# Weight sign and softmax-sum steps moved between engines, and the value product of a group issued in one piece

## The chip, the cores and the metric

The kernel runs on one core of one Trainium2 chip. Five engines matter. TensorE (PE in the profile, with its weight loads as PEld) multiplies matrices out of SBUF into PSUM. VectorE (DVE) and ScalarE (ACT) work elementwise on SBUF and PSUM. GpSimd (POOL) works elementwise on SBUF only. SyncE (SP) issues most of the DMAs. The metric is the device time of one execution in microseconds; lower is better.

## The reference

Three stages follow one another. In the kernel's sizes: 4 batches, 8 heads, sequence 576, head dimension 64; then 2304 tokens of width 512.

```python
scores = scale * np.matmul(q, k.transpose(0, 1, 3, 2)) + bias   # bias: a small MLP of log distances
attn = np.exp(scores - np.max(scores, axis=-1, keepdims=True))
attn = attn / (np.sum(attn, axis=-1, keepdims=True) + 1e-09)
x = np.matmul(attn, v)                       # heads side by side: (2304, 512)
h = x @ w_in                                 # d_ff 2048
g = (a0 + a1*h + a2*h*h + a3*h*h*h) / (1 + |b0|*|h| + |b1|*h*h + 1e-6)
x = g @ w_out
h = np.maximum(np.maximum(x @ w1, x @ w2), x @ w3)   # d_ff 768
out = h @ w_out2
```

The six weight matrices of the last two stages arrive as 64-bit floats; everything else is 32-bit.

## The kernel before

**Attention.** A pair of heads `p` (four of them) of batch `b` is cut into five row blocks `t` of 128 rows (the last has 64 rows of each head, so one block serves both heads). One `(b, t, p)` is a unit; there are 80. `attn_tick(n)` (L719) issues, in the order of the list `A2`, one step each for several units at once: `scores` of unit n (L223, PE, into two PSUM buffers called `wide`, one for each head), `reduce_min` of unit n (L258, DVE: adds the bias, scales, finds the row minimum; it frees the `wide` buffer), `expo` of unit n (L264, ACT, with the row sum), `normalise` of unit n-1 (L266), `transposes` of unit n-2 (L287, PE, into `bank` buffers, of which there are four) and their copies to SBUF on ACT and DVE. For 14 of the 16 pairs `(b, p)` the units run t = 0 to 4 in two groups, [0, 1] and [2, 3, 4]. I call these five ticks a cycle.

**Softmax sum.** `normalise` adds 1e-9 to the two sums `st` (128x2), takes the reciprocal in place and spreads it to a 128x128 tile `rb`, which PE transposes into `tt` (L303) as the last matmul of the unit's transposes. All three steps are on DVE (`NE` is 'd').

**Value product.** When the last block of a group has been transposed, `attn_v` (L323) is queued for the next ticks: ten matmuls (`av`) whose moving operand is the whole group, 256 or 320 columns. They are cut into pieces of one tick each by `cuts` (L765): for a group of two blocks j = 0..2 and then 3..4, for a group of three j = 0..1, 2..3 and 4. `attn_store` (L340) then scales the result out of its bank on DVE.

**Weights.** A weight of 64-bit floats is loaded as pairs of 32-bit words, `low` and `high` (L371). `rebias` (L379) multiplies the high word, read as a 32-bit float, by 2^-112 on ACT and shifts the low word right by 29 on DVE; `join` (L385) makes `(high << 3) | low` on DVE; `sign` (L390) takes the sign bit of the high word and ors it in, on DVE. `parts` (L402) then splits the result into a rounded and a remaining part, on ACT and on POOL or DVE. Sixteen weights `wi` are narrowed during attention and written back to DRAM (`wnwin`), sixteen `wo` are prepared around the start of the first feed-forward block, and 24 of the last stage (`m0`, `m1`, `m2`, `mo`) from the last feed-forward block on, one for each step. That makes 56 such weights in all.

**Feed-forward.** `ffn_tick` (L669) runs 16 steps for each of five token blocks. A step has 12 matmuls `ph`, 12 matmuls `y` of the step two before, the rational function on ACT and DVE (`rat_poly`, `rat_inv`, `rat_newton`) and its split `gs` (ACT, then POOL, L507), followed by one step of the weight pipeline. `moe_tick` (L813) runs the last stage.

**What sets the order.** In attention from tick 8 on, PE and SP run in the order of the program, while the order of DVE, ACT and POOL is chosen by a scheduler at build time. In the feed-forward stage DVE, too, runs in the order of the program. Each engine executes its own queue strictly in that order.

Of the kernel before, what the change touches and what calls it, by code (L numbers as in the profile page):

```python
# [13 lines left out]
ALU = mybir.AluOpType  # L14
# [23 lines left out]
def tile_attention_moe(  # L38
# [328 lines left out]
    def weight_stages(src, name, n, packed=False, lo_eng=pool, narrow=None):  # L367
# [11 lines left out]
        def rebias():  # L379
            if wide_:  # L380
                low, high = box["r"][:, :, 0], box["r"][:, :, 1]
                act.activation(f32(high), f32(high), AF.Copy, scale=REBIAS)
                dve.tensor_scalar(low, low, 29, None, ALU.logical_shift_right)  # L383

        def join():  # L385
            if wide_:
                low, high = box["r"][:, :, 0], box["r"][:, :, 1]
                dve.scalar_tensor_tensor(low, high, 3, low, ALU.logical_shift_left, ALU.bitwise_or)  # L388

        def sign():  # L390
            if wide_:
                low, high = box["r"][:, :, 0], box["r"][:, :, 1]
# [3 lines left out]
                dve.scalar_tensor_tensor(res, high, SIGN, low, ALU.bitwise_and, ALU.bitwise_or)  # L396
# [498 lines left out]
```

## Time and profile before

| | |
|---|---|
| median of three runs | 1100.29 us (1100.19 to 1100.94) |
| profiled execution, its own time | 1100.39 us |
| its span, first to last instruction | 1098.6 us |
| around the span | 1.8 us |
| PE busy | 1040.5 us (95%) |
| DVE busy | 750.8 us (68%) |
| ACT busy | 620.7 us (57%) |
| POOL busy | 418.9 us (38%) |

The shares are means over stages with different limits. Attention fills about 45 to 360 us of the span (after a first part that builds the bias), the feed-forward blocks 360 to 800, and the last stage 800 to the end. A busy PE in this profile is not PE at its full rate, since a matmul that waits in the middle counts as busy, so starts of groups on the timeline say more than the busy share.

### The profile page before, as it was taken

To read this page: it belongs to the slowest core of one execution; us is meant where nothing else is said; L and a number is where in the kernel's file an instruction comes from. 1 tells how busy PE (TensorE), PEld (TensorE's weight loads), DVE (VectorE), ACT (ScalarE), POOL (GpSimd) and SP (SyncE) were. 2 spreads that over 40 slices of the span, in tenths; PEclk is the share of its full clock that TensorE was granted. 3 is DMA by queue.
4 is the path that set the end of the run, shared out by engine and by line. 5 is a ranking of instruction groups with operands and counts; after the bars stand their busy time and mean duration, and the time that the engine had idled before them with its cause. 6 is when DMAs were issued, how large, how long until landed. Compare 5 with 4: busy or idle time off the path is not lost. (4 is left out here: it accounts for less than half of the span.)

```text
span 1098.6 us, 16477 instructions
## 1 busy us (share of the span) xinstructions
PE 1040.5 (95%) x5996; PEld 811.5 (74%) x5996; DVE 750.8 (68%) x1512; ACT 620.7 (57%) x1226; POOL 418.9 (38%) x409
## 2 busy tenths in 40 slices
PE   5699999999999879999999999999999999999998
PEld 2247677677776557878889788777688788888887
DVE  8496899899998899877789777799984211111111
ACT  5686667676778667766678766777632211211111
POOL 7614555455486534322233323243442330211111
PEclk9799999999999889999999999999999999999999
DMA  7486845255455422010020200223233200201010
GB/s 261 158 314 217 291 153 168 99 204 173 155 160 174 136 103 77 1 58 1 1 77 1 78 1 1 78 77 115 77 118 131 77 1 1 77 1 58 1 39 20
DMA packets 43393, 107.94 MB, mean 98 GB/s; under 512 B 4784, under 2 KB 11184, under 8 KB 43312
## 3 DMA queue, kind: packets, MB, share of 16 engines
q1 hardware_dynamic: 38128, 96.27, 26.1%
q10 hardware_dynamic: 5184, 10.62, 2.5%
q8 instruction: 47, 0.77, 0.3%
q14 instruction: 34, 0.28, 0.1%
HBM read 77.90 MB, written 28.97 MB: 97 GB/s over the span
## 5 line engine op out<-in xcount | busy, mean ns | idle before, releaser
L459 PE MATMUL p<-ys,wm 128*128 128x512 f32 (+1 forms) x1080 | 228.8, 369 | 2.8 <-POOL wm L413 1.8
L459 PE MATMUL ph<-xs,wwi 128*128 128x512 f32 (+1 forms) x960 | 217.8, 375 | 5.7 <-ACT at L748 3.5
L459 PEld LDWEIGHTS p<-ys,wm 128*128 128x128 f32 x1080 | 188.4, 188 | 39.4 <-POOL wm L413 2.2
L459 PE MATMUL y<-gs,wwo 128*128 128x512 f32 (+1 forms) x905 | 207.7, 374 | 7.9 <-POOL gs L507 7.2
L459 PEld LDWEIGHTS ph<-xs,wwi 128*128 128x128 f32 x960 | 170.4, 191 | 41.8 <-POOL xs L451 3.8
L507 POOL TENSOR_TENSOR gs<-g,gs 128x512 fp32r<-128x512 f32 (+1 forms) x80 | 102.2, 1277 | 234.6 <-ACT gs L506 160.2
L459 PEld LDWEIGHTS y<-gs,wwo 128*128 128x128 f32 x905 | 157.3, 188 | 46.4 <-POOL gs L507 13.7
L264 ACT ACTIVATE e<-e,st 128x576 f32<-128x576 f32 x144 | 111.5, 775 | 59.3 <-DVE st L258 53.4
L551 POOL TENSOR_TENSOR h2s<-mx,h2s 128x512 fp32r<-128x512 f32 (+1 forms) x30 | 35.9, 1197 | 226.9 <-ACT h2s L550 226.9
L258 DVE CUSTOM_DVE_ANT_0 e<-s,bias 128x576 f32<-128x576 f32 x144 | 104.0, 751 | 16.3 <-PE s L233 11.7
L547 DVE TENSOR_TENSOR mx<-p,mx 128x512 f32<-128x512 f32 (+1 forms) x30 | 19.1, 637 | 140.0 <-PE p L459 136.1
L480 ACT ACTIVATE s<-ph,keep 128x512 f32<-128x512 f32 (+1 forms) x80 | 49.3, 617 | 75.9 <-PE ph L459 74.1
L233 PE MATMUL s<-k,qs 128*128 128x288 f32 x512 | 86.3, 308 | 4.6 <-DVE st L258 2.8
L550 ACT CAST h2s<-mx 128x512 fp32r<-128x512 f32 (+1 forms) x30 | 17.3, 578 | 128.9 <-DVE mx L548 128.9
L296 PEld LDWEIGHTS tp<-ident,e 128*128 128x128 f32 x576 | 62.5, 142 | 35.6 <-issue 17.1
L296 PE MATMUL tp<-ident,e 128*128 128x128 f32 x576 | 82.0, 282 | 1.0 <-DVE at L317 0.8
L482 DVE SCALAR_TENSOR_TENSOR g<-g,keep,s 128x512 f32<-128x512 f32 (+1 forms) x80 | 55.2, 690 | 36.6 <-ACT g L481 36.0
L338 PE MATMUL av<-at,v 128*64 128x320 f32 (+3 forms) x576 | 77.7, 392 | 1.3 <-DVE st L269 0.7
L565 PE MATMUL o<-wmo,h2s 128*128 128x512 f32 x324 | 78.6, 390 | 0.0
L233 PEld LDWEIGHTS s<-k,qs 128*128 128x128 f32 x512 | 70.6, 189 | 9.0 <-DVE st L258 3.7
L185 PE MATMUL pb<-h,keep 128*32 128x288 f32 x576 | 48.7, 442 | 23.8 <-ACT h L173 22.6
L487 ACT ACTIVATE s<-g,keep 128x512 f32<-128x512 f32 (+1 forms) x80 | 52.7, 659 | 31.7 <-DVE g L482 31.6
(102 smaller groups left out, 1665.0 us busy)
## 6 DMA issues: line engine op xcount, KB each, us to landing
bias_d<-bo ACTq DMA_DIRECT2D x36, 288.0 KB, 2.9
kr<-in_k SPq DMA_DIRECT2D x16, 576.0 KB, 5.1
qr<-in_q SPq DMA_DIRECT2D x16, 576.0 KB, 5.6
bias<-bias_d SPq DMA_DIRECT2D x16, 576.0 KB, 5.3
wrm<-in_m SPq DMA_DIRECT2D x18, 512.0 KB, 3.6
wrwin<-in_wi SPq DMA_DIRECT2D x16, 512.0 KB, 4.4
wrwo<-in_wo SPq DMA_DIRECT2D x16, 512.0 KB, 3.7
v<-in_v SPq DMA_DIRECT2D x8, 576.0 KB, 4.5
```

Of the source, the lines that this page charges most:

```text
L185: pe.matmul(pb[32 * c:32 * c + 32, x, :HS], lhsT=hw_sb, rhs=hs[c][:, x * HS:(x + 1) * HS], start=True, stop=True,)
L233: pe.matmul(pt[:, x, :HS], lhsT=qs[:, u, t * P:(t + 1) * P], rhs=ks[u][:, w, x * HS:(x + 1) * HS], start=w == 0, stop=w == 1,)
L258: dve.tensor_tensor_reduce(out=dst, in0=src, in1=bs, op0=ALU.add, op1=ALU.min, scale=-0.125, scalar=3.0e38, accum_out=st[:, u:u + 1],)
L264: act.activation(et[:, u], et[:, u], AF.Exp, bias=st[:, u:u + 1], scale=-1.0, accum_out=st[:, 2 + u:3 + u])
L296: pe.transpose(tp[:, j * P:(j + 1) * P], flat[:, 640 * u + j * P:640 * u + (j + 1) * P], ident)
L338: pe.matmul(po[r, :n], lhsT=l, rhs=m, start=j == 0, stop=j == 4, skip_group_check=True)
L459: pe.matmul(po, lhsT=wpart(key, a, k), rhs=rhs, start=first and i == 0, stop=last and i == 2)
L480: act.activation(s, ph, AF.Abs, scale=B0)
L482: dve.scalar_tensor_tensor(q, q, B1, s, ALU.mult, ALU.add)
L487: act.activation(s, q, AF.Ln, bias=qcol)
L507: pool.tensor_tensor(t[1], u, f32(t[0]), ALU.subtract)
L565: pe.matmul(po, lhsT=h[:, a, tt * P:(tt + 1) * P], rhs=w[c], start=j == 0 and i == 0, stop=j == NF2 - 1 and i == 2,)
```

## The change

Three edits are made together. First, `rebias` uses the activation Prelu with slope -2^32 for negative values instead of Copy: a negative high word comes out positive and 2^32 times larger, which sets exactly the bit that the shift by three moves into the sign. `sign` falls away, and `join` writes the final result; for a narrowed weight the store follows `join` at once, so its list of stages is one shorter. Second, in `normalise` the addition of 1e-9 and the spreading to `rb` go to POOL; the reciprocal stays on DVE between them. Third, `CUT2` and `CUT3` become 1, so each group's ten `av` matmuls stand in one tick.

```diff
...
-'CUT2': 2, 'CUT3': 3,
+'CUT2': 1, 'CUT3': 1,
...
-SIGN = -(1 << 31)
+TOSIGN = -2.0 ** 32
...
-        dve.tensor_scalar(r, r, 1e-9, None, ALU.add)
+        pool.tensor_scalar(r, r, 1e-9, 0.0, ALU.add, ALU.add)
+        dve.reciprocal(r, r)
         rb = sb.tile([P, 2, 64], F32, tag="rb", name=f"rb{b}_{t}_{p}", bufs=4)
-        dve.reciprocal(r, r)
-        evac(KN["NE"], (rb, r.unsqueeze(2).to_broadcast([P, 2, 64])))
+        pool.tensor_copy(rb, r.unsqueeze(2).to_broadcast([P, 2, 64]))
...
-                act.activation(f32(high), f32(high), AF.Copy, scale=REBIAS)
+                act.activation(f32(high), f32(high), AF.Prelu, scale=REBIAS, alpha=TOSIGN)
                 dve.tensor_scalar(low, low, 29, None, ALU.logical_shift_right)
...
         def join():
-            if wide_:
-                low, high = box["r"][:, :, 0], box["r"][:, :, 1]
-                dve.scalar_tensor_tensor(low, high, 3, low, ALU.logical_shift_left, ALU.bitwise_or)
-
-        def sign():
             if wide_:
...
-                dve.scalar_tensor_tensor(res, high, SIGN, low, ALU.bitwise_and, ALU.bitwise_or)
+                dve.scalar_tensor_tensor(res, high, 3, low, ALU.logical_shift_left, ALU.bitwise_or)
                 box["r"] = f32(res)
...
-            return [load, rebias, join, lambda: (sign(), put())]
-        return [load, rebias, lambda: (join(), sign()), parts]
+            return [load, rebias, lambda: (join(), put())]
+        return [load, rebias, join, parts]
...
-        eq += st[1:3] + [st[0] for st in early[i + 2:i + 3]] + st[3:]
+        eq += st[1:2] + [st[0] for st in early[i + 2:i + 3]] + st[2:]
```

On PE, at the first two ticks of the pair b = 1, p = 3 (`s` are scores, `tp` and `tt` transposes; the numbers behind a name are t and p, and for `s` and `tp` the half), this stood in a row before:

```order
L233 MATMUL s_0_3_0_2457<-k_3_0_2207,qs_3_2206 128x288 x4
L233 MATMUL s_0_3_1_2462<-k_3_1_2208,qs_3_2206 128x288 x4
L338 MATMUL av_0_2_2467<-at_0_2_2221,v_2_1744 64x256 x6
L296 MATMUL tp_3_2_0_2474<-ident,e_3_2_2359 128x128 x4
L296 MATMUL tp_3_2_1_2479<-ident,e_3_2_2359 128x128 x4
L302 MATMUL tt_3_2_2484<-ident,e_3_2_2359 128x128
L303 MATMUL tt_3_2_2484<-ident,rb_3_2_2433 128x128
L233 MATMUL s_1_3_0_2504<-k_3_0_2207,qs_3_2206 128x288 x4
L233 MATMUL s_1_3_1_2509<-k_3_1_2208,qs_3_2206 128x288 x4
L338 MATMUL av_0_2_2467<-at_0_2_2221,v_2_1744 64x256 x2
L338 MATMUL av_0_2_2467<-att_0_2_2222,v_2_1744 64x256 x2
L296 MATMUL tp_4_2_0_2518<-ident,e_4_2_2405 128x128 x4
```

And this stands there now:

```order
L233 MATMUL s_0_3_0_2464<-k_3_0_2214,qs_3_2213 128x288 x4
L233 MATMUL s_0_3_1_2469<-k_3_1_2215,qs_3_2213 128x288 x4
L296 MATMUL tp_3_2_0_2474<-ident,e_3_2_2359 128x128 x4
L296 MATMUL tp_3_2_1_2479<-ident,e_3_2_2359 128x128 x4
L302 MATMUL tt_3_2_2484<-ident,e_3_2_2359 128x128
L303 MATMUL tt_3_2_2484<-ident,rb_3_2_2442 128x128
L233 MATMUL s_1_3_0_2504<-k_3_0_2214,qs_3_2213 128x288 x4
L233 MATMUL s_1_3_1_2509<-k_3_1_2215,qs_3_2213 128x288 x4
L296 MATMUL tp_4_2_0_2514<-ident,e_4_2_2402 128x128 x4
```

No `av` stands between scores and transposes in these two ticks any more; all ten matmuls of group [0, 1] now stand in the tick of t = 4 and all ten of [2, 3, 4] in the tick of t = 2 of the next pair, so that the ticks of t = 0, 1 and 3 have none.

On POOL, for the same place (`qs` and `k` are the split of the next pair's queries and keys, `e` the copy of the last block's tail), this stood in a row before:

```order
L138 TENSOR_SCALAR qs_0_2440<-qr_0_2219 128x1024
L144 TENSOR_SCALAR k_0_0_2441<-kr_0_2217 128x576
L141 TENSOR_TENSOR qs_0_2440<-qr_0_2219,qs_0_2440 64x512 x2
L275 COPY e_4_2_2405<-e_4_2_2405 128x64
L147 TENSOR_TENSOR k_0_0_2441<-kr_0_2217,k_0_0_2441 128x576
```

And this stands there now:

```order
L272 COPY rb_2_2_2391<-st_2_2_2309 128x128
L138 TENSOR_SCALAR qs_0_2447<-qr_0_2226 128x1024
L144 TENSOR_SCALAR k_0_0_2448<-kr_0_2224 128x576
L269 TENSOR_SCALAR st_3_2_2360<-st_3_2_2360 128x2
L141 TENSOR_TENSOR qs_0_2447<-qr_0_2226,qs_0_2447 64x512 x2
L269 TENSOR_SCALAR st_4_2_2403<-st_4_2_2403 128x1
L275 COPY e_4_2_2402<-e_4_2_2402 128x64
L147 TENSOR_TENSOR k_0_0_2448<-kr_0_2224,k_0_0_2448 128x576
L272 COPY rb_3_2_2442<-st_3_2_2360 128x128
L272 COPY rb_4_2_2491<-st_4_2_2403 128x128
```

The spread `rb` of unit t = 3, which PE needs in the first tick of the next pair, now stands behind three large splits that lie between it and its own addition.

On DVE, at the same ticks (`e`, `st` are the reductions of unit t, `xs` the store of a group), this stood in a row before:

```order
L258 ISA e_0_3_2455,st_0_3_2456<-s_0_3_0_2457,bias_3_1319 128x576
L258 ISA st_0_3_2456 128x1
L269 TENSOR_SCALAR st_4_2_2406<-st_4_2_2406 128x1
L271 RECIPROCAL st_4_2_2406<-st_4_2_2406 128x1
L317 COPY rb_4_2_2490<-st_4_2_2406 128x128
L258 ISA e_1_3_2502,st_1_3_2503<-s_1_3_1_2509,bias_3_1361 128x576
```

And this stands there now:

```order
L258 ISA e_0_3_2462,st_0_3_2463<-s_0_3_0_2464,bias_3_1317 128x576
L258 ISA st_0_3_2463 128x1
L270 RECIPROCAL st_4_2_2403<-st_4_2_2403 128x1
L258 ISA e_1_3_2502,st_1_3_2503<-s_1_3_1_2509,bias_3_1367 128x576
```

Of the three steps only the reciprocal is left on DVE, and it waits for POOL.

## Rows read from the trace of the kernel before

**Rows 1.** By stretch: length, busy (count) of PE, PEld, DVE, ACT, POOL; clock, DMA.

```profile
200.00:350.00 150.00, 149.03 (x1099) 109.85 (x1097) 135.11 (x383) 112.52 (x265) 90.72 (x108) 1.00 0.50 167
...
355.00:405.00 50.00, 39.73 (x169) 28.36 (x170) 44.36 (x71) 33.87 (x62) 22.82 (x17) 0.86 0.41 136
...
700.00:795.00 95.00, 90.09 (x375) 69.03 (x373) 89.81 (x134) 69.50 (x120) 36.79 (x25) 1.00 0.31 100
```

**Rows 2.** PE timeline of a steady attention cycle: start, duration, engine, line, group.

```profile
230.83 1.53 PE L243 MATMUL s<-k,qtail 128*128 128x512 f32 x8
...
235.28 1.52 PE L338 MATMUL av<-at,v 128*64 128x256 f32 x12
236.73 1.09 PE L296 MATMUL tp<-ident,e 128*128 128x128 f32 x8
...
237.79 1.30 PE L233 MATMUL s<-k,qs 128*128 128x288 f32 x8
239.03 0.65 PE L338 MATMUL av<-at,v 128*64 128x256 f32 x4
...
240.19 0.66 PE L296 MATMUL tp<-ident,e 128*128 128x128 f32 x4
...
240.82 1.29 PE L233 MATMUL s<-k,qs 128*128 128x288 f32 x8
...
247.87 1.53 PE L243 MATMUL s<-k,qtail 128*128 128x512 f32 x8
```

**Rows 3.** Groups by line and shape, 100 to 340 us: count, busy us, mean ns.

```profile
L264 ACT ACTIVATE e<-e,st 128x576 f32<-128x576 f32 x120 | 92.9, 775 | 54.8 <-DVE st L258 49.0 <-DVE st L269 4.3 <-ACT att L315 1.3
L258 DVE CUSTOM_DVE_ANT_0 e<-s,bias 128x576 f32<-128x576 f32 x121 | 87.0, 750 | 11.6 <-PE s L233 7.3 <-PE s L243 3.6 <-issue 0.4
...
L147 POOL TENSOR_TENSOR k<-kr,k 128x576 fp32r<-128x576 f32 x26 | 37.6, 1447 | 1.2
L141 POOL TENSOR_TENSOR qs<-qr,qs 64x512 fp32r<-64x512 f32 x26 | 35.3, 1376 | 1.1
...
L317 DVE COPY rb<-st 128x128 f32<-128x128 f32 x69 | 30.7, 444 | 2.3
...
L269 DVE TENSOR_SCALAR st<-st 128x2 f32<-128x2 f32 x53 | 19.6, 369 | 0.4 <-ACT e L264 0.4
```

**Rows 4.** Timelines of DVE and POOL at one normalisation.

```profile
243.73 1.05 DVE L269 TENSOR_SCALAR st<-st 128x2 f32<-128x2 f32 x1
...
243.71 1.04 POOL L138 TENSOR_SCALAR qs<-qr 128x1024 fp32r<-128x1024 f32 x1
```

**Rows 5.** PE timeline, the longest of eight waits between 100 and 200 us.

```profile
114.06 1.47 PE L233 MATMUL s<-k,qs 128*128 128x288 f32 x8 [1.74 <-DVE st L258]
```

**Rows 6.** Timelines of ACT and PE around the first feed-forward steps.

```profile
363.76 0.68 ACT L412 CAST wwo<-wrwo 128x512 fp32r<-128x512 f32 x1 [2.44 <-DVE wrwo L396]
...
389.30 1.22 PE L459 MATMUL y<-gs,wwi 128*128 128x512 f32 x2 [4.78 <-ACT gs L506]
```

**Rows 7.** PE and DVE timelines of the last feed-forward block.

```profile
700.31 2.96 PE L459 MATMUL y<-gs,wwo 128*128 128x512 f32 x12
...
705.84 2.95 PE L459 MATMUL y<-gs,wwo 128*128 128x512 f32 x12
...
784.64 3.31 PE L459 MATMUL y<-gs,wwo 128*128 128x512 f32 x12
...
722.13 0.75 DVE L494 SCALAR_TENSOR_TENSOR g<-g,keep,s 128x512 f32<-128x512 f32 x1
...
728.01 0.75 DVE L494 SCALAR_TENSOR_TENSOR g<-g,keep,s 128x512 f32<-128x512 f32 x1
...
735.60 0.75 DVE L494 SCALAR_TENSOR_TENSOR g<-g,keep,s 128x512 f32<-128x512 f32 x1
```

**Rows 8.** Two lines by themselves: count, then min/median/max ns.

```profile
L396 DVE SCALAR_TENSOR_TENSOR wrm<-wrm x18: 681/693/1669, 713.1 to 841.2; 128x512 int32<-128x512 int32 x18
...
L507 POOL TENSOR_TENSOR gs<-g,gs x15: 1290/1539/1818, 703.0 to 790.6; 128x512 fp32r<-128x512 f32 x15
```

More of the change, by code (lines that the diff above doesn't have):

```diff
@@ L29 @@
 TW = 1148
-KN = {'NSLOT': 35, 'NRAW': 3, 'NRAWX': 2, 'NATT': 4, 'HB': 0, 'NE': 'd', 'FP': 2, 'BL': 4, 'T4': 0, 'LSP': 1, 'KX': 4, 'HT': 'ss', 'EVP': 'da', 'TTP': 'dda', 'NXS': 4, 'EARLY': 0, 'NM0': 8, 'MAN': 2, 'MANF': 3, 'A1': ['b', 'T', 'sc', 'st', 'r0', 'av', 'b', 'b', 'b', 'sq', 'n', 'r1', 'p2', 'v0', 'v1', 'e0', 'e1'], 'A2': ['sc', 'av', 'p1', 'T', 'r1', 'r0', 'n', 'st', 'p2', 'sq', 'e0', 'e1', 'v0', 'v1'], 'LL': 10, 'SL': 4, 'LL0': 9, 'SL0': 4, 'SQ': [2, 1, 1], 'CUT2': 2, 'CUT3': 3, 'WS': 9, 'WE': 70, 'WT': 61, 'XT': 8, 'XA': 3, 'XB': 8, 'F': ['g2a', 'g2d', 'h', 'g1a', 'w', 'g2p', 'g1d', 'g1p', 'y', 'x', 'g3'], 'LOW': 4, 'LOM': 3, 'LOI': 0, 'GHI': 'dve', 'GLO': 'dve', 'BED': 8, 'BE0': 16, 'NU1': 'pool', 'XE': ['act', 'pool'], 'WR': 1, 'YSP': 'act', 'LAG': 2, 'EV1': 'dve', 'XSE': 'act', 'STQ': 'sp', 'PUQ': 'sp', 'NB0': 0, 'HP': 0, 'SB': 2, 'XLA': 3, 'XLB': 6, 'XSA': 11, 'YL': 10, 'YS': 14, 'WLOW': 1}
+KN = {'NSLOT': 35, 'NRAW': 3, 'NRAWX': 2, 'NATT': 4, 'HB': 0, 'NE': 'd', 'FP': 2, 'BL': 4, 'T4': 0, 'LSP': 1, 'KX': 4, 'HT': 'ss', 'EVP': 'da', 'TTP': 'dda', 'NXS': 4, 'EARLY': 0, 'NM0': 8, 'MAN': 2, 'MANF': 3, 'A1': ['b', 'T', 'sc', 'st', 'r0', 'av', 'b', 'b', 'b', 'sq', 'n', 'r1', 'p2', 'v0', 'v1', 'e0', 'e1'], 'A2': ['sc', 'av', 'p1', 'T', 'r1', 'r0', 'n', 'st', 'p2', 'sq', 'e0', 'e1', 'v0', 'v1'], 'LL': 10, 'SL': 4, 'LL0': 9, 'SL0': 4, 'SQ': [2, 1, 1], 'CUT2': 1, 'CUT3': 1, 'WS': 9, 'WE': 70, 'WT': 61, 'XT': 8, 'XA': 3, 'XB': 8, 'F': ['g2a', 'g2d', 'h', 'g1a', 'w', 'g2p', 'g1d', 'g1p', 'y', 'x', 'g3'], 'LOW': 4, 'LOM': 3, 'LOI': 0, 'GHI': 'dve', 'GLO': 'dve', 'BED': 8, 'BE0': 16, 'NU1': 'pool', 'XE': ['act', 'pool'], 'WR': 1, 'YSP': 'act', 'LAG': 2, 'EV1': 'dve', 'XSE': 'act', 'STQ': 'sp', 'PUQ': 'sp', 'NB0': 0, 'HP': 0, 'SB': 2, 'XLA': 3, 'XLB': 6, 'XSA': 11, 'YL': 10, 'YS': 14, 'WLOW': 1}
 REBIAS = 2.0 ** -112
-SIGN = -(1 << 31)
+TOSIGN = -2.0 ** 32
 QC = 1.0 + 1e-6
```

## The prediction

> **What bounds the kernel now.** I read the busy time by stretch first, then the PE timeline of the stretches where PE is full, then the engine that ends PE's waits where it is not.
>
> From 200 to 350 us PE is busy 149.03 of 150 us and DVE 135.11, while POOL has 90.72 [rows 1]. One attention cycle of five units takes 247.87 - 230.83 = 17.04 us [rows 2], and its groups follow one another without a gap. So in steady attention PE sets the time, and what DVE sheds there gains nothing by itself. DVE is close behind, though, and its small operations cost more than their size: the addition takes 369 ns and the spreading to `rb` 444 ns on average [rows 3].
>
> It is different in three places. Between 100 and 200 us PE waits eight times, 4.8 us in sum, mostly on DVE; the longest wait is 1.74 us for the reduction that frees a score buffer [rows 5]. From 355 to 405 us PE is busy for only 39.73 of 50 us and DVE for 44.36 [rows 1]; ACT waits 2.44 us for a `sign`, and PE 4.78 us for a chain that has come through DVE [rows 6]. In the last feed-forward block, 700 to 795 us, DVE has 89.81 of 95 us [rows 1]. A step at PE's pace is 705.84 - 700.31 = 5.53 us, and 14 steps would be 77.4; they take 784.64 - 700.31 = 84.33 [rows 7], so 6.9 us are lost. DVE's own steps there are 5.88 us, and every third is 735.60 - 728.01 = 7.59 [rows 7].
>
> **The change part by part.**
>
> *The sign in the last block.* One operation of 0.69 us (median) [rows 8] leaves DVE per step. Three DVE steps were 2 x 5.88 + 7.59 = 19.35 us; they become 19.35 - 3 x 0.69 = 17.28, against 16.59 for PE. If the long step still holds PE up, 0.69 us in three steps stays lost, 2.3 us over the ten steps that lose time, and the gain is 4.6. If PE's lead of two steps absorbs it, the gain is the whole 6.9. I take -6 us; bounds -4.5 to -7.
>
> *The sign around the first block.* Sixteen signs, 11 us of DVE, go from 355 to 440 us. Where a `sign` holds up ACT's next cast, as at 363.76 us [rows 6], everything behind it on ACT moves up by 0.69 us: the copies that free PE's banks as well as the first `gs`. But part of this stretch waits for weight loads, which the change doesn't speed. I take -5; bounds -9 to -1.
>
> *The early waits.* DVE loses 0.37 + 0.44 = 0.81 us for each unit [rows 3] where it holds PE up. I take 4 of the 4.8 us; bounds 0 to -4.8.
>
> *Fewer pieces of the value product.* Twelve passes of 256 columns take 236.73 - 235.28 = 1.45 us, and two groups of four 240.19 - 239.03 = 1.16, so 0.58 each [rows 2]. A pass is then (1.45 - 0.58) / 8 = 0.109 us and the start of a group 0.58 - 4 x 0.109 = 0.145. Each value product loses one start, two in a cycle, 0.29 us; over 14 cycles -4.1 us. PE is the bound here, so this counts in full.
>
> *Uneven ticks.* Scores take 239.03 - 237.79 = 1.24 us, transposes 237.79 - 236.73 = 1.06, those of the last block 240.82 - 240.19 = 0.63 [rows 2]. Without `av` the ticks of t = 0, 1 and 3 are 2.30, 1.87 and 2.30 us long for PE; those with a burst are about 5.3 (t = 2) and 5.0 (t = 4). The sum, 16.8, is the old cycle less 0.29. In the tick of t = 1 PE is ready for the next scores 0.63 us after the last ones end, but the reduction that frees the first buffer takes 0.75 [rows 3], and signals come on top. I estimate 0.3 us of waiting, at least 0.12. If DVE still has the copies of the tick before in its queue (the order of one cycle has some 1.7 us of them between two reductions), it is up to 1.3.
>
> *`rb` on POOL.* The new order puts the `rb` of unit t = 3 behind two splits of 1.376 us and one of 1.447 [rows 3]. From the start of that unit's scores PE asks for this `rb` after the rest of the tick (2.30), the tick of t = 4 (5.0), and the scores and first transposes of the next pair (1.24 + 0.95): 9.5 us. On the other side: scores 1.24, two reductions 1.5, two exponentials 1.55 [rows 3], and on ACT a copy or so between them, 4.3 to 5.2, say 5.0. Then POOL: the three splits 4.2, and the two additions, the tail's copy and `rb` itself. POOL has no such small operation in these rows; between nothing and its 1.04 for 1024 columns [rows 4] I put the four together at 1.1 (bounds 0.5 to 2), nearer to the low end, since they have 2 to 128 columns. That gives 10.3, and PE waits 0.8 us; bounds 0 to 1.9. On DVE the reciprocals wait for POOL's additions, and queued behind them are stores and copies, which then fall into a burst of PE. I count nothing for that; if the cover goes, it is inside the 1.9.
>
> The two waits overlap in part: while PE waits for `rb`, DVE clears its queue, and the other wait shrinks to its 0.3. Together I take 1.05 us a cycle, 14.7 us over 14 cycles; bounds 0.1 to 2.0, 1.4 to 28 us.
>
> *At no cost.* Prelu takes Copy's place on the same 512 columns of ACT, which has 37 us free in 150 [rows 1]. POOL takes about 0.5 us more for each unit, 22 us for the 44 units from 200 to 350 us, and had 59 free [rows 1]; it is the place in its queue that counts, not the load.
>
> *A rule beside a row.* DVE's addition at 243.73 us took 1.05 us, as long as POOL's operation beside it, 243.71 to 244.75 [rows 4]. The Trainium skill, page "SBUF — State Buffer", section "SBUF: two separate sides", says that VectorE and GpSimd share a port pair which an operation holds to its end while the other engine blocks. This row agrees. By that rule the four small POOL operations could each be held up in turn by a DVE operation of 0.4 to 0.7 us, and `rb` would come up to 2 us later. The sum goes by the rows above; this possibility is part of the second rival.
>
> The sum: -6 - 5 - 4 - 4.1 + 14.7 = -4.4. The profiled execution took 1100.39 us (its span 1098.6), 0.1 above the median of the runs. I predict **1096.0 us**.
>
> **The rivals.**
>
> *The bursts cost nothing.* If DVE, now relieved of a quarter of its work in attention (44 x 0.81 of 135 us), keeps pace in the light ticks and `rb` comes in time, a cycle loses only the 0.3: 1100.4 - 19.1 + 4.2 = 1085.5. For it speaks that PE's cycle had no wait before, with DVE at 90% [rows 1]; against it that the light tick of 1.87 us is shorter than anything PE had.
>
> *POOL holds PE up.* The place is the transpose of `rb` of unit t = 3 in the tick of t = 0. If POOL's small operations wait for DVE, as the `gs` splits in the last block do (1.54 us in the median, 1.29 at best [rows 8]), each cycle loses 2.0 us: 1100.4 - 19.1 + 28 = 1109. It decides from 19.1 / 14 = 1.37 us a cycle; above that the kernel is slower than before. For it speaks the order, in which the splits stand ahead of `rb` in 12 of the 14 cycles; against it that nothing else is urgent on POOL.
>
> *The relief of DVE does not reach PE.* If weight loads and POOL's `gs` take over as the bound in both feed-forward places, their -11 shrinks to -3, and the time is 1096 + 8 = 1104.
>
> **How the numbers follow.** The forecast (waits of 0.6 to 1.5 us a cycle, 1090 to 1102) has 0.47, the free bursts 0.25, POOL 0.16, the missing relief 0.12. A measurement of this kernel tells about 0.2% (2.2 us) from no change. Faster by more than that (below 1098.1) is most of the forecast (0.37) and the free bursts (0.25): 0.62. Within 0.2% are 0.08 of the forecast and 0.05 of the others: 0.13. Slower is the rest, 0.25. The range that leaves 0.2 out runs from 1083, below the free bursts, to 1107, into POOL's case. The likeliest case's own range is 1090 to 1102.
>
> **What would show it.** After: no DVE operation between `join` and the split; the last block's `y` groups 5.5 to 5.8 us apart and DVE at about 80 of 95 us there; PE above 42 of 50 us from 355 to 405; in attention a cycle of about 17.8 us, with PE waits named after POOL's `rb` at the last transpose and after DVE's reduction at the scores of t = 2. A cycle of 16.8 to 17.1 would prove the burst free, one of 18.5 or more would prove the queue on POOL decisive; steps of 6 us or more in the last block would refute the first term.

## The result, and the profile after

The change makes the kernel 0.8% faster: 1091.48 us in the median of four runs (1090.14 to 1092.50) against 1100.42 us (1100.19 to 1100.94) before. The ratio is 0.9917 with a 95% interval of 0.990 to 0.9935. The gain is 8.9 us where 4.4 was forecast. The profiled execution took 1091.77 us, its span 1090.0.

Busy time by stretch after, with the columns and stretches of [rows 1]:

```profile
200.00:350.00 150.00, 136.25 (x985) 105.77 (x982) 93.77 (x260) 99.26 (x232) 105.27 (x181) 0.97 0.47 151
355.00:405.00 50.00, 45.19 (x245) 32.84 (x244) 38.40 (x76) 41.66 (x83) 27.80 (x33) 0.93 0.43 133
700.00:795.00 95.00, 95.00 (x415) 77.42 (x414) 88.22 (x132) 76.26 (x130) 40.92 (x31) 1.00 0.33 106
```

In attention PE is no longer full: 136.25 of 150 us against 149.03, although DVE's busy time there has fallen by 41 us (135.11 to 93.77; some of it because fewer units fall into the stretch). In the last feed-forward block it is full, 95.00 against 90.09. So the change loses in the first stage and gains in the others. Four points of PE's timeline cut the span into stages: the start of the last scores of a tail (the 128x512 matmuls, one group in each cycle), of the first `y` of the last block, of the first `p` of the last stage, and the span's end. They are read from one traced execution of each kernel. The last two columns are experiments from the next section.

| starts, us | before | after | s_only | s_first |
|---|---|---|---|---|
| last tail scores of attention | 351.02 | 366.83 | 347.92 | 347.39 |
| last block's first `y` | 694.22 | 697.72 | 680.18 | 679.73 |
| first `p` | 787.79 | 783.99 | 766.42 | 773.28 |
| end of the span | 1098.6 | 1090.0 | 1072.2 | 1086.1 |

Attention is 15.8 us longer after. The stretch from there to the last block is 12.3 us shorter (330.89 against 343.20), the last block 7.3 (86.27 against 93.57), the last stage 4.8. Together -8.6.

The PE timeline of a cycle after, which answers [rows 2]: start, duration, engine, line, group, in brackets the wait before it and what ended it.

```profile
107.12 1.53 PE L243 MATMUL s<-k,qtail 128*128 128x512 f32 x8
...
232.28 1.56 PE L243 MATMUL s<-k,qtail 128*128 128x512 f32 x8
...
241.09 0.33 PE L303 MATMUL tt<-ident,rb 128*128 128x128 f32 x1 [1.52 <-POOL rb L272]
...
243.34 1.47 PE L233 MATMUL s<-k,qs 128*128 128x288 f32 x8 [0.20 <-DVE st L258]
...
250.96 1.56 PE L243 MATMUL s<-k,qtail 128*128 128x512 f32 x8
...
305.30 1.56 PE L243 MATMUL s<-k,qtail 128*128 128x512 f32 x8
...
326.40 1.55 PE L243 MATMUL s<-k,qtail 128*128 128x512 f32 x8
...
337.74 0.47 PE L303 MATMUL tt<-ident,rb 128*128 128x128 f32 x1 [3.42 <-POOL rb L272]
...
349.70 1.56 PE L243 MATMUL s<-k,qtail 128*128 128x512 f32 x8
```

This cycle takes 250.96 - 232.28 = 18.68 us, where [rows 2] had 17.04. It has two waits: for POOL's `rb` in the tick of t = 0, and at the scores of t = 2 for the reduction that frees their buffer. The eleven cycles from 107.12 to 305.30 average 18.02 us; the same eleven before averaged 17.69 (104.36 to 298.97). Then come two of 21.10 and 23.30.

POOL's timeline beside the wait at 241.09:

```profile
235.47 3.04 POOL L141 TENSOR_TENSOR qs<-qr,qs 64x512 fp32r<-64x512 f32 x2
238.59 1.41 POOL L147 TENSOR_TENSOR k<-kr,k 128x576 fp32r<-128x576 f32 x1
240.08 0.23 POOL L269 TENSOR_SCALAR st<-st 128x1 f32<-128x1 f32 x1
240.37 0.24 POOL L275 COPY e<-e 128x64 f32<-128x64 f32 x1
240.54 0.50 POOL L272 COPY rb<-st 128x128 f32<-128x128 f32 x1
```

`rb` stands behind 4.45 us of splits, as the order showed. Groups after, by line and shape, 100 to 340 us, which answer [rows 3]:

```profile
L258 DVE CUSTOM_DVE_ANT_0 e<-s,bias 128x576 f32<-128x576 f32 x114 | 82.4, 754 | 29.2 <-PE s L233 23.8 <-PE s L243 5.1
...
L272 POOL COPY rb<-st 128x128 f32<-128x128 f32 x64 | 20.9, 331 | 42.8 <-DVE st L270 40.0 <-PE tt L302 2.5
L269 POOL TENSOR_SCALAR st<-st 128x2 f32<-128x2 f32 x50 | 11.5, 229 | 13.6 <-ACT e L264 10.9
```

DVE's reductions had waited 11.6 us for something, now 29.2, both nearly all for PE: DVE has the time, but PE doesn't use it. The `y` groups of the last block, which answer [rows 7]:

```profile
703.83 2.95 PE L454 MATMUL y<-gs,wwo 128*128 128x512 f32 x12
...
781.20 2.95 PE L454 MATMUL y<-gs,wwo 128*128 128x512 f32 x12
```

Fourteen steps take 77.37 us where they took 84.33: PE's pace of 5.53 throughout.

### The profile page after: what moved, and what is told of

It is laid out like the page before. It is cut to its first block, busy times and chain, and to the rows that moved or that the text cites. A ratio compares the mean times of both kernels' runs of the same rounds, so it can differ in the third digit from the quotient of the medians.

```text
span 1090.0 us, 16451 instructions
## 1 busy us (share of the span) xinstructions
PE 1032.2 (95%) x5996; PEld 818.8 (75%) x5996; DVE 658.4 (60%) x1296; ACT 624.4 (57%) x1226; POOL 449.8 (41%) x569
## 5 line engine op out<-in xcount | busy, mean ns | idle before, releaser
L454 PE MATMUL y<-gs,wwo 128*128 128x512 f32 (+1 forms) x905 | 204.1, 372 | 1.3 <-POOL gs L502 1.1
L502 POOL TENSOR_TENSOR gs<-g,gs 128x512 fp32r<-128x512 f32 (+1 forms) x80 | 95.8, 1197 | 234.4 <-ACT gs L501 168.0
L258 DVE CUSTOM_DVE_ANT_0 e<-s,bias 128x576 f32<-128x576 f32 x144 | 104.3, 755 | 40.3 <-PE s L233 34.2
L264 ACT ACTIVATE e<-e,st 128x576 f32<-128x576 f32 x144 | 111.3, 775 | 20.2 <-DVE st L258 15.8
L542 DVE TENSOR_TENSOR mx<-p,mx 128x512 f32<-128x512 f32 (+1 forms) x30 | 19.1, 637 | 141.3 <-PE p L454 137.4
L233 PE MATMUL s<-k,qs 128*128 128x288 f32 x512 | 90.5, 317 | 4.3 <-DVE st L258 2.7
L233 PEld LDWEIGHTS s<-k,qs 128*128 128x128 f32 x512 | 74.1, 197 | 11.6 <-DVE st L258 5.1
L296 PEld LDWEIGHTS tp<-ident,e 128*128 128x128 f32 x576 | 65.6, 142 | 17.5 <-issue 13.1
L477 DVE SCALAR_TENSOR_TENSOR g<-g,keep,s 128x512 f32<-128x512 f32 (+1 forms) x80 | 55.3, 692 | 37.8 <-ACT g L476 36.3
L743 ACT COPY at<-tp 128x512 f32<-128x512 f32 x80 | 46.5, 584 | 52.1 <-PE tp L296 52.0
L338 PE MATMUL av<-at,v 128*64 128x320 f32 (+3 forms) x576 | 72.0, 387 | 0.4 <-ACT at L743 0.4
```

The source lines that it names most:

```text
L233: pe.matmul(pt[:, x, :HS], lhsT=qs[:, u, t * P:(t + 1) * P], rhs=ks[u][:, w, x * HS:(x + 1) * HS], start=w == 0, stop=w == 1,)
L258: dve.tensor_tensor_reduce(out=dst, in0=src, in1=bs, op0=ALU.add, op1=ALU.min, scale=-0.125, scalar=3.0e38, accum_out=st[:, u:u + 1],)
L264: act.activation(et[:, u], et[:, u], AF.Exp, bias=st[:, u:u + 1], scale=-1.0, accum_out=st[:, 2 + u:3 + u])
L296: pe.transpose(tp[:, j * P:(j + 1) * P], flat[:, 640 * u + j * P:640 * u + (j + 1) * P], ident)
L338: pe.matmul(po[r, :n], lhsT=l, rhs=m, start=j == 0, stop=j == 4, skip_group_check=True)
L454: pe.matmul(po, lhsT=wpart(key, a, k), rhs=rhs, start=first and i == 0, stop=last and i == 2)
```

## The experiments

Times are medians, ratios stand against the kernel before on the same chip. A cycle is the mean of fourteen, between the first and the last full one's start, before 17.62 and after 18.55 us. The runs come from several chips, on which the kernel before took 1097.2 to 1100.4 us in the median; so a difference of up to some 3 us between two medians is not shown by them alone. Where it matters I give the difference of the gains as well, each against the kernel before on its own chip.

| label | us | ratio, 95% interval | cycle, us |
|---|---|---|---|
| s_only | 1074.0 | 0.978 (0.976 to 0.981) | 17.32 |
| n_only | 1105.2 | 1.007 (1.004 to 1.009) | 17.73 |
| c_only | 1115.7 | 1.016 (1.014 to 1.019) | 18.72 |
| s_c | 1089.7 | 0.993 (0.990 to 0.995) | 18.31 |
| s_n | 1086.3 | 0.990 (0.988 to 0.992) | 17.82 |
| s_first | 1085.5 | 0.989 (0.985 to 0.993) | 17.33 |
| s_cut2 | 1080.5 | 0.985 (0.981 to 0.989) | 17.58 |
| s_noadd | 1070.7 | 0.975 (0.972 to 0.979) | 17.10 |
| s_c_noadd | 1083.9 | 0.988 (0.984 to 0.992) | 17.84 |
| s_half | 1071.9 | 0.978 (0.976 to 0.980) | 17.02 |
| s_c_half | 1084.8 | 0.989 (0.987 to 0.991) | 18.16 |
| s_c_nea | 1083.8 | 0.988 (0.984 to 0.992) | 17.52 |
| s_evp | 1078.2 | 0.981 (0.979 to 0.984) | 17.40 |
| s_c_evp | 1077.0 | 0.982 (0.978 to 0.986) | 17.58 |
| a_loi | 1091.5 | 0.993 (0.991 to 0.996) | 18.41 |
| a_late | 1085.9 | 0.988 (0.985 to 0.991) | 18.06 |
| s_n_late | 1078.0 | 0.981 (0.978 to 0.984) | 17.30 |
| s_noadd_half | 1070.6 | 0.975 (0.972 to 0.977) | 17.07 |

**The three edits apart.** `s` is the sign, `n` the normalisation, `c` the burst. s_only is the change without the other two:

```diff
-'CUT2': 1, 'CUT3': 1,
+'CUT2': 2, 'CUT3': 3,
...
-        pool.tensor_scalar(r, r, 1e-9, 0.0, ALU.add, ALU.add)
-        dve.reciprocal(r, r)
+        dve.tensor_scalar(r, r, 1e-9, None, ALU.add)
...
-        pool.tensor_copy(rb, r.unsqueeze(2).to_broadcast([P, 2, 64]))
+        dve.reciprocal(r, r)
+        evac(KN["NE"], (rb, r.unsqueeze(2).to_broadcast([P, 2, 64])))
```

s_c has only the second part of this diff, s_n only the first; n_only and c_only are the kernel before with that one edit of the change.

s_only: 

> The weight sign alone; normalisation and pieces of the value product as before. Theory 'sum': the three edits add up, and the changed kernel's -12.3 us around the first feed-forward block, -7.3 in the last block and -4.8 on the way into the last stage all belong to the sign, with attention as before: about 1076 us. Rival 'given back': the changed kernel loses 9.7 us in two long attention cycles near the end, in which the weight preparation runs on, so that about 7 of the 12.3 us are only that loss returned; then the sign alone gains about 5 + 7 + 5 = 17 us: about 1083 us.

n_only: 

> The softmax-sum steps on POOL alone. Theory 'sum': all of the 15.8 us that the changed kernel loses in attention come from the transpose of rb that waits for POOL (16.3 us of PE's idle time there): about 1116 us. Rival 'given back': the first block returns some 7 of them: about 1109 us. If the value product in small pieces covers rb's lateness (the light ticks then have 0.6 us and more of other work), it is below 1103 us.

c_only: 

> The value product in one piece alone, with DVE still loaded by sign and normalisation. Theory 'the burst is free': about 1096 us (the 4 us of group starts). Rival 'DVE cannot keep pace in the light ticks': 0.3 to 1.3 us a cycle and more, 1104 to 1118 us, with PE waits at the scores of t = 2.

s_c: 

> Sign and value product in one piece, normalisation on DVE as before, so POOL's queue is as before. Theory 'sum' with POOL as the whole cause of the loss in attention: about 1074 to 1077 us. If the light ticks cost what DVE's queue asks, 1080 to 1090 us. 'Given back' puts it at 1083 us or more with a first block that gains about 5 us.

s_n: 

> The sign edit and the normalisation on GpSimd, the value product in pieces as before. Theory that the place of `rb` in GpSimd's queue has a price of its own, whatever the ticks look like: the normalisation alone cost 6.6 us, so 1074 + 5 to 7, 1079 to 1081 us, with waits of the last transpose on GpSimd's `rb`. Rival, that its price and the relief of VectorE's queue nearly cancel, as between the run with bursts and the full change (1089.7 and 1091.5): 1074 to 1077.

The sign alone gains 24.6 us by the medians. In the table of starts, whose two traces differ by 26.4, attention is 3.1 us shorter, the stretch behind it 10.9, the last block 7.3, the last stage 5.0. No other edit takes that back later: what n_only and c_only lose, they lose in attention. The burst alone costs 17.1 us, and 15.7 on top of the sign. That is more than forecast, and GpSimd's queue is as before in these two, so it cannot be the cause there. The normalisation alone costs 6.6 us, which none of the three cases for n_only named, and 12.3 on top of the sign (13.6 by the gains), against both theories for s_n. Both together cost 17.5 on top of the sign (1091.5 - 1074.0; 15.6 by the gains), not 28: they overlap. On top of the burst the normalisation adds next to nothing (1089.7 to 1091.5; by the gains nothing). The overlap shows in the traces: in the full change PE's waits in attention are for `rb` (15.1 us from 105 to 365 us) and hardly for DVE's reductions (2.3), in s_c for DVE's reductions and copies (12.5). In s_n, without bursts, `rb` costs nothing in the eleven cycles (188.4 us against 188.2 in s_only); the price is at the start (+3.4), in the last three cycles (+6.7) and behind attention (+1.9).

**Where the sign's gain lies.** s_first keeps the old third operation for the weights of the last stage:

```diff
+        keep = name[0] == "m"
...
+                if keep:
+                    dve.scalar_tensor_tensor(res, high, SIGN, low, ALU.bitwise_and, ALU.bitwise_or)
```

> Only the sign edit, and of it only what lies around the first feed-forward block and before: the weights `wi` and `wo` are signed on ScalarE, those of the last stage (`m0`, `m1`, `m2`, `mo`) by the old third operation on VectorE. With the sign removed everywhere the trace had attention 3.1 us shorter than before, the stretch from the last attention scores to the last block 10.9 us, the last block 7.3 and the last stage 5.0. Theory that each gain belongs to the weights prepared in its own stretch: the first two stay (14 us), the last two go, so about 1085.5 us (1083 to 1088), with the last block again 93.6 us and the rest 311. Rival, that the last stage gains because everything in front of it starts in better order: the last stage keeps its 5 us, and the time is about 1080.5.

In the trace the theory holds to the tenth in the table of starts: 332.34 us to the last block, like s_only's 332.26, and a last block of 93.55 like the 93.57 before. The last stage loses its gain too (312.8 us against 310.8 before). That trace is of a run of 1087.9 us; of the four runs two took 1088 and two 1083, and where the faster ones save 5 us is not shown. How DVE's 24 removed operations reach the last stage is seen on PE there, before:

```profile
855.89 2.56 PE L459 MATMUL p<-ys,wm 128*128 128x512 f32 x10 [1.78 <-POOL wm L413]
```

The same place in s_first:

```profile
841.84 3.71 PE L461 MATMUL p<-ys,wm 128*128 128x512 f32 x10 [1.78 <-POOL wm L415]
```

And after, in one group without a stop:

```profile
841.31 8.52 PE L454 MATMUL p<-ys,wm 128*128 128x512 f32 x36
```

PE waits there for the split of a weight that came late through DVE's three stages. With two stages it comes in time.

**Why the burst costs.** One burst instead of two, for the groups of two blocks:

```diff
-'CUT2': 2, 'CUT3': 3,
+'CUT2': 1, 'CUT3': 3,
```

> The sign edit, and only the groups of two blocks in one burst; those of three in pieces as before. Then one tick of a cycle (t = 1) has no value product, instead of three with both bursts. Theory that the price comes with each light tick and that the one behind another light tick is the dearest: about 3 to 6 of the 15.7 us, less 2 us for the starts of groups that fall away: 1074 to 1079 us. Rival, that a single light tick is covered by VectorE's lead: 1070 to 1073, faster than the sign edit alone. Rival, that the two-block burst carries the whole price: 1086 to 1090.

A steady cycle is 17.36 us in nearly every instance, 0.32 above 17.04 although a start of a group falls away. So one light tick isn't covered, but costs little: over 14 cycles 4.5 us of the 6.5 measured, which is just above the range of the theory. The next five take away either an operation of DVE or the hold of GpSimd on it.

The addition left out:

```diff
-        dve.tensor_scalar(r, r, 1e-9, None, ALU.add)
```

s_noadd: 

> The sign edit alone, value product in pieces, and the addition of 1e-9 left out (it falls under the rounding of a sum that is at least 1). It takes 0.35 us per unit from VectorE's queue and puts nothing in its place. The control for the run with bursts and without this addition. If TensorE sets the cycle when the value product comes in pieces, only the early waits shrink: 1070 to 1074 us. If VectorE's queue sets the cycle there too, 80 units x 0.35 = 28 us bound the gain, and the time is 1050 to 1065.

s_c_noadd: 

> The sign edit, the value product as a burst, VectorE's normalisation as before but the addition of 1e-9 left out. Theory that the burst costs its 15.7 us because VectorE falls behind in the three light ticks of a cycle: 0.35 us less in each of them is up to 1 us a cycle, 14.7 us in 14 cycles; so 1075 to 1083 us, and the waits of scores on VectorE's reductions fall by half at least. Rival, that the light ticks are held up by something else (the exponentials on ScalarE, the banks, the signals between engines): no more gain than in the run with pieces, 1086 to 1090 us.

GpSimd's subtractions in halves:

```diff
-            pool.tensor_tensor(ks[u][:, 1], kr[:, u], f32(ks[u][:, 0]), ALU.subtract)
+            for c in (slice(0, 288), slice(288, 576)):
+                pool.tensor_tensor(ks[u][:, 1, c], kr[:, u, c], f32(ks[u][:, 0, c]), ALU.subtract)
...
+            for c in (slice(0, 256), slice(256, 512)):
+                lo_eng.tensor_tensor(qs[low, u, c], qr[low, u, c], f32(qs[low, u, c]), ALU.subtract)
```

s_half: 

> The sign edit alone, with GpSimd's subtractions of the splits of queries and keys (1.4 us each) cut into two halves by columns: no work less, two instructions for one. The control for the run with bursts. The value product stands in pieces, TensorE sets most cycles at 17.04 us, and shorter operations on GpSimd can only help where a cycle is longer than that: 1069 to 1074 us. If shorter operations on GpSimd help everywhere, 1060 to 1068.

s_c_half: 

> The sign edit, the bursts, and GpSimd's subtractions of the splits cut into halves. In the run with bursts every second cycle of the trace took 19.3 to 19.9 us and the others 17.4 to 17.7. In a long one VectorE's addition took 1.38 us and the weight's shift 1.43, against medians of 0.16 and 0.42, and both ended with a subtraction on GpSimd. Theory that these holds make the long cycles: halves hold at most 0.7 us, the long cycles shrink to 18.2 to 18.6, and 1089.7 falls by 6 to 9, to 1081 to 1084 us. Rival, that the long cycles come from VectorE's own weight steps, which fall into every second cycle: 1088 to 1091, long cycles unchanged.

The addition left out, and `rb` copied by ScalarE:

```diff
-'NE': 'd',
+'NE': 'a',
...
-        dve.tensor_scalar(r, r, 1e-9, None, ALU.add)
```

s_c_nea: 

> The sign edit, the bursts, the addition of 1e-9 left out and the spreading to `rb` on ScalarE, so that of the normalisation only the reciprocal stays on VectorE, which took 0.16 to 0.17 us in every execution, beside GpSimd or not. Theory that it is GpSimd's hold on VectorE's small operations that makes the long cycles: nothing but the weight steps can be held now, all cycles are near 17.4 us, and the time is 1074 to 1079, against 1083.9 with `rb` on VectorE. Rival, that ScalarE, which has 66 us free in 240 and takes some 25 more, now delays the exponentials and with them the transposes: 1084 to 1095.

With bursts each gains 5 to 6 us (3.5 to 5.2 by the gains); without them the missing addition gains 3.3 and the halves 2.1 (2.7 and 0.7 by the gains, so for the halves only the shorter cycle in the table speaks). s_c_noadd ended between its theory and its rival, s_c_half just above its theory's range. s_c_nea settles nothing by its time (1078.3 to 1088.4 us over its runs), and none brings the burst's price to zero. The theory that GpSimd's holds make the long cycles has fallen as the whole cause: with halves, cycles of 19.1 to 19.8 us are left. What makes them shows in s_c, on PE:

```profile
212.20 1.55 PE L243 MATMUL s<-k,qtail 128*128 128x512 f32 x8 [0.39 <-DVE st L258]
...
215.25 1.94 PE L338 MATMUL av<-at,v 128*64 128x256 f32 x14 [0.92 <-DVE at L317]
...
224.33 1.49 PE L233 MATMUL s<-k,qs 128*128 128x288 f32 x8 [1.27 <-DVE st L258]
...
232.07 1.56 PE L243 MATMUL s<-k,qtail 128*128 128x512 f32 x8
...
241.78 1.47 PE L233 MATMUL s<-k,qs 128*128 128x288 f32 x8 [0.41 <-DVE st L258]
```

and on DVE before the scores that wait at 224.33:

```profile
221.99 0.68 DVE L391 SCALAR_TENSOR_TENSOR wnwin<-wrwin 128x512 int32<-128x512 int32 x1
222.59 0.68 DVE L317 COPY at<-tp 128x512 f32<-128x512 f32 x1
223.19 0.41 DVE L317 COPY att<-tt 128x256 f32<-128x256 f32 x1
223.52 0.74 DVE L258 CUSTOM_DVE_ANT_0 e<-s,bias 128x576 f32<-128x576 f32 x1
```

The reduction that the scores need starts after a weight step and two copies; at 215.25 the burst itself waits for a copy `at` on DVE. The copy `at` (0.68 us) goes to DVE in every second tick (`EVP`, by parity), and a cycle has five ticks. So DVE has it in three of the four ticks of one cycle that make one, and in one of the next. In the first kind of cycle the copy of t = 0 falls into a light tick, in the other that of t = 3. s_c_evp and its control s_evp deal it out by the place in the cycle, to DVE in the two ticks with a burst:

```diff
-'EVP': 'da',
+'EVP': 'aadad',
```

s_c_evp: 

> The sign edit and the bursts, and the second copy of each transposed block dealt out between VectorE and ScalarE by the place in the cycle instead of by tick parity: five ticks make a cycle, so by parity VectorE has it in three of the four ticks of one cycle and in one of the next; now it has it in the two ticks with a burst, always. Theory that this copy (0.68 us) in the light tick of t = 0 makes every second cycle 2 us longer: all cycles 17.3 to 17.7 us, 1089.7 less about 12, so 1076 to 1080. Rival, that the weight steps on VectorE make the long cycles: 1087 to 1091, with cycles above 19 us left.

s_evp: 

> The sign edit and the copies dealt out by the place in the cycle, the value product in pieces: the control for the run with bursts. TensorE sets the cycle at 17.04 us; only the longer first cycles can shrink: 1070 to 1075 us.

PE in s_c_evp, two cycles of 17.32 and 17.71 us:

```profile
192.19 1.55 PE L243 MATMUL s<-k,qtail 128*128 128x512 f32 x8
...
209.51 1.55 PE L243 MATMUL s<-k,qtail 128*128 128x512 f32 x8
...
219.49 1.48 PE L233 MATMUL s<-k,qs 128*128 128x288 f32 x8 [0.69 <-DVE st L258]
227.22 1.55 PE L243 MATMUL s<-k,qtail 128*128 128x512 f32 x8
```

The alternation is gone and 12.7 of the 15.7 us with it (12.2 by the gains), though DVE's weight steps, the rival, are all left; the control moved by 4 us the other way, above its range, and why is open. So most of the burst's price without POOL's `rb` comes from the copies that DVE has in the light ticks. Even so the burst gains nothing: 17.58 us a cycle against 17.32 in s_only and 17.40 in s_evp, and 1077.0 us against 1078.2 in s_evp on the same chip, which is no difference by these runs.

**Why the normalisation costs.** a_loi is the full change with the low parts of the weights `wi` made on DVE instead of GpSimd:

```diff
-'LOI': 0,
+'LOI': 1,
```

> The full change, with the low parts of the narrowed weights `wi` made on VectorE instead of GpSimd (16 operations in the last cycles of attention). Theory that the normalisation on GpSimd costs where `rb` stands behind these operations: the two cycles of 21.1 and 23.3 us before the end of attention become 17.5 to 18.5, the waits of the last transpose on `rb` fall from 15.1 us to below 8, and 1091.5 falls by 6 to 9, to 1082 to 1086. Rival, that those cycles are long from VectorE's or ScalarE's weight steps: no gain or a loss from VectorE's extra 16 x 0.7 us or more, 1090 to 1100.

a_late is the full change, s_n_late the run s_n, both with the normalisation back on DVE in the last batch:

```diff
+        e_ = pool if b < 3 else dve
...
-        pool.tensor_copy(rb, r.unsqueeze(2).to_broadcast([P, 2, 64]))
+        e_.tensor_copy(rb, r.unsqueeze(2).to_broadcast([P, 2, 64]))
```

a_late: 

> The full change, with the normalisation back on VectorE in the last of the four batches only (the last four cycles of attention, where the weights `wi` are split). Theory that the normalisation on GpSimd costs most where the weights' splits share GpSimd's queue: the last three cycles take 54 to 57 us, as in the run with sign edit and bursts (54.5), instead of 61.5; the time is 1083 to 1087. Rival, that the last cycles are long by the weights themselves: 1090 to 1093.

s_n_late: 

> The sign edit and the normalisation on GpSimd, pieces, and the normalisation back on VectorE in the last batch. With it on GpSimd throughout the last three cycles took 61.1 us against 54.4 with the sign edit alone. Theory as in the run with bursts: they fall back to 54 to 56 us, and 1086.3 becomes 1079 to 1081. Rival: no change, 1085 to 1087.

In a_loi the waits for `rb` (105 to 365 us) fell from 15.1 to 11.2 us, but those for DVE's reductions rose from 2.3 to 6.8: half of the theory, and no gain. a_late confirms the place: the last three cycles take 55.3 us instead of 61.5, and the time falls by 5.6 (4.7 by the gains). Without bursts they take 54.1 instead of 61.1, and the time falls by 8.3 (10.6 by the gains). POOL's timeline after, ahead of the wait that ends at 337.74:

```profile
331.50 1.28 POOL L408 TENSOR_TENSOR wwi<-wrwi,wwi 128x512 fp32r<-128x512 f32 x1
332.86 2.50 POOL L141 TENSOR_TENSOR qs<-qr,qs 64x512 fp32r<-64x512 f32 x2
335.44 1.40 POOL L147 TENSOR_TENSOR k<-kr,k 128x576 fp32r<-128x576 f32 x1
...
337.39 0.29 POOL L272 COPY rb<-st 128x128 f32<-128x128 f32 x1
```

A weight's split has joined those of queries and keys ahead of `rb`. That these splits alone make the cycles long is not shown, since a_loi, which takes them away, loads DVE instead.

**Both helpful edits without bursts:** s_noadd_half joins s_noadd and s_half. 

> The sign edit, the value product in pieces, the addition of 1e-9 left out and GpSimd's subtractions in halves: the two edits that helped without bursts, together. Each took 2 to 3 us off the sign edit's 1074, both by early cycles that were longer than 17.04 us. If they worked on the same waits, 1069 to 1072; if they add, 1067 to 1069.

The two don't add, as they wouldn't if they worked on the same waits. This kernel and s_noadd are the fastest found, 2.5% below the kernel before and 1.9% below the change (by their medians).

## Why the prediction was right or wrong

The direction was right and the size was half of what came. The steps that failed are the sign's terms: the one around the first block was taken at -5, and the one in the last stage at nothing. The terms, with what they measured:

| term | forecast | measured |
|---|---|---|
| sign, last block | -6 (-4.5 to -7) | -7.3 |
| sign, around the first block | -5 (-9 to -1) | -12.3 (s_only -10.9) |
| sign, last stage | none | -4.8 |
| first cycle's start | none | +2.8 |
| eleven cycles | +4.4 | +3.6 |
| last three cycles | +2.3 | +9.5 |
| sum | -4.4 | -8.6 |

The forecast of the cycles is its early waits (-4) and, for each, 1.05 - 0.29 us.

The sign gained 13.4 us more than forecast, and attention lost 9.2 us more. These misses nearly cancel, so it is luck that the time lies within the range given for the likeliest case.

**The last block** was right. PE's lead absorbs even the long step, and the gain is the whole loss of [rows 7] (it falls into the seven steps from 739 us on, not into ten). DVE is still busy for 88 of 95 us, not 80: the same stretch now holds more steps.

**Around the first block** the step that failed is "part of this stretch waits for weight loads, which the change doesn't speed". The first half was right: before, DVE stood for 3.83 us for a load, its queue behind it, and the wait of 4.78 us in [rows 6] follows on that.

```profile
383.30 0.43 DVE L383 TENSOR_SCALAR wrwo<-wrwo 128x512 int32<-128x512 int32 x1 [3.83 <-DMA wrwo<-in_wo]
```

The second half was wrong: DVE's waits for these loads fall from 4.7 us before (355 to 440 us) to 1.3 in s_only (350 to 430), and PE's wait for `gs` from 4.78 to 0.77. SP issues such a load when a staging buffer is free, and before it waited there above all for POOL's splits that free one (`wwo`, L413: 31.2 us from 355 to 440). These come behind `sign`. That the shorter chain brings the loads forward is argued, not tested. Later DVE itself is the bound. Busy time before, a view that the prediction did not read beyond 405 us:

```profile
365.00:385.00 20.00, 17.27 (x68) 11.87 (x68) 16.00 (x27) 14.49 (x26) 7.93 (x6) 0.83 0.48 145
385.00:405.00 20.00, 14.71 (x53) 11.46 (x54) 19.05 (x30) 13.27 (x24) 7.54 (x5) 0.83 0.36 134
405.00:425.00 20.00, 19.09 (x82) 15.05 (x81) 18.18 (x28) 13.32 (x26) 6.46 (x8) 1.00 0.23 80
425.00:445.00 20.00, 18.76 (x80) 14.48 (x79) 19.34 (x31) 15.49 (x28) 9.02 (x7) 1.00 0.07 26
```

and PE's waits there, on work that has come through DVE:

```profile
398.19 1.19 PE L459 MATMUL ph<-xs,wwi 128*128 128x512 f32 x4 [0.99 <-DVE g L490]
...
410.92 2.82 PE L459 MATMUL y<-gs,wwo 128*128 128x512 f32 x11 [0.90 <-POOL gs L507]
...
429.09 2.82 PE L459 MATMUL y<-gs,wwo 128*128 128x512 f32 x11 [1.15 <-POOL gs L507]
```

After, its `y` groups there follow at 5.53 us without a wait (405.32, 410.85 and so on). In s_only and s_first this stretch gains 10.9 us, close to the 11.0 of sixteen operations of 0.69 us; but removed work, earlier loads and PE's clock all differ (the clock granted was 0.83 from 385 to 405 us before, 1.00 from 378 to 398 us in s_only), and the runs don't part them. The other 1.4 us of the -12.3 come with the other two edits and stay open.

**The last stage** was left out of the sum. Twenty-four signs were counted only in the block before it, though the weights go on there; the trace of s_first shows that they are the cause.

**The steady cycle** was right in its mechanism, at the place of `rb`, and nearly in its size. Ten waits for `rb` from 132.96 to 295.43 sum to 9.1 us, 0.91 a cycle where 0.8 was forecast, at the place named, behind the splits named. The four small operations of POOL take 0.23 + 0.23 + 0.24 + 0.50 = 1.20 us in that cycle (0.99 with the median `rb`, 0.29), where 1.1 was taken. The reduction adds 0.20 where 0.3 was taken. This price needs both edits, since s_n's eleven cycles don't have it. The 0.29 us for fewer pieces show in no run: behind the first full cycle no kernel with both bursts has one below 17.1 us, while those with pieces have 17.03.

**The early waits** were under-read. The six cycles from 104.36 us before last 18.18 us on average, 6.8 us more in all than at 17.04, where the waits counted in [rows 5] sum to 4.8. The change takes 1.8 us from these six, and adds 1.07 us to each of the next five. In s_only the six are 6.3 us shorter than before: DVE loses seven `sign` operations there too (16 in all of attention), which the sum put at nothing.

**The last three cycles** fell out of the step that multiplies by 14: it took a steady cycle for all. At the end POOL also splits `wi`, and `rb` waits longer; a_late gives 5.6 us of it back. This is the second rival's place, in two cycles and not in all, but not its cause: ahead of the wait POOL's small operations take their usual 0.23 to 0.29 us, behind one split more. The start (+2.8 us) appears in every kernel with the normalisation on POOL, with bursts or not (the first full cycle starts at 106.8 to 108.8 us, in s_only, c_only and s_c at 104.3 to 105.4). Of the 2.8 us, 1.2 are a wait for POOL's `rb` at 75.70 us, in the part that builds the bias. The rest lies between two tails, 5.52 us apart where it was 3.95; its cause is open, and s_c_nea, with `rb` on ACT, also starts at 106.8.

Of the rivals, "the bursts cost nothing" is refuted by the eleven cycles of 18.02 us, where s_n has 17.13 with pieces, "POOL holds PE up" is true only at the end, and "the relief of DVE does not reach PE" is refuted by s_only. What none of them said is that the burst costs as much without POOL's `rb` (s_c, 15.7 us), by the wait of up to 1.3 us for DVE's queue that the prediction named as a bound and didn't take.

## What to carry to other kernels

Where an engine that runs in program order is busy for 95% of a stretch, count a removed operation at its full duration for every issue there, ask whether waits beside it, here for loads, hang on the same chain, and follow the operation into every other stage. A price per cycle holds for the cycles that look alike; read the first and the last ones by themselves. When the work of one engine is bunched, ask which work of the others is dealt out by a different period: here, without POOL's `rb`, most of the burst's price came where a copy dealt out by parity fell into a light tick.

## What was not expected of the hardware

The same small operation of DVE takes very different times beside POOL. Its line before, then two of s_c, 105 to 345 us: count, then min/median/max ns.

```profile
L269 DVE TENSOR_SCALAR st<-st x68: 142/164/1140, 106.6 to 343.2; 128x2 f32<-128x2 f32 x53, 128x1 f32<-128x1 f32 x15
...
L269 DVE TENSOR_SCALAR st<-st x65: 142/163/1384, 106.5 to 343.5; 128x2 f32<-128x2 f32 x51, 128x1 f32<-128x1 f32 x14
L271 DVE RECIPROCAL st<-st x65: 162/166/168, 106.7 to 343.7; 128x2 f32<-128x2 f32 x51, 128x1 f32<-128x1 f32 x14
```

The addition is held at times: the one in [rows 4] ended with POOL's operation, and one of 1.38 us in s_c, begun at 212.75 us, with a subtraction of POOL that ended at 214.10. The reciprocal of the same columns never is. So the 369 ns of [rows 3], on which the prediction built its early waits, is a median of 0.16 us and some long holds. That the next operation would be held in its place is not shown: without the addition, `rb` took 512 ns in the mean (s_noadd) against 494 (s_only). With POOL's subtractions in halves the longest addition took 942 ns (s_c_half). The Trainium skill, page "SBUF — State Buffer", section "SBUF: two separate sides", says that the loser of the shared port pair blocks until the other's operation ends; these rows agree.

The clock followed the late waits. Busy time after, by two microseconds, around the wait that ended at 337.74:

```profile
332.00:334.00 2.00, 2.00 (x19) 2.00 (x18) 1.06 (x2) 1.50 (x4) 1.92 (x2) 1.00 0.96 273
334.00:336.00 2.00, 0.31 (x3) 0.07 (x1) 0.81 (x4) 0.39 (x1) 1.92 (x3) 1.00 0.55 156
...
338.00:340.00 2.00, 2.00 (x10) 1.98 (x10) 0.42 (x1) 0.97 (x3) 2.00 (x4) 0.50 0.01 4
...
344.00:346.00 2.00, 2.00 (x16) 0.90 (x14) 1.15 (x5) 1.58 (x4) 1.26 (x4) 1.00 0.44 131
```

After the stop the granted clock was 0.50 (1.2 GHz). On PE's timeline, eight score matmuls of one shape ahead of the stop, and eight behind it:

```profile
332.03 1.30 PE L233 MATMUL s<-k,qs 128*128 128x288 f32 x8
...
341.23 2.27 PE L233 MATMUL s<-k,qs 128*128 128x288 f32 x8
```

So a wait of 3.4 us cost more than itself: its cycle took 23.30 us, 5.3 more than the mean of the eleven, with 3.8 us of waits in it. Prelu costs ScalarE what Copy did: 0.68 us in the median for 128x512, on `wm` before and after.
